# Retention and gMLP block: the first pair's half-row block last, five w_sg transposes instead of ten, a new order

## Chip, core and metric

One core of one Trainium2 chip. The metric is device time in microseconds; less is better.

## What is computed

```python
scores = (1 / sqrt(64)) * q @ k^T             # q, k, v: 8 sequences x 8 heads x 576 x 64, float32
ret = scores * where(t >= s, gamma_h ** (t - s), 0)
x = ret @ v                                   # joined over heads: 8 x 576 x 512
h = gelu_tanh(x @ w_in)                       # 512 -> 1024; u, v = the two halves of 512
v_n = (v - mean) / sqrt(var + 1e-6) * g_ln
v_s = einsum('ts,bsd->btd', w_sg, v_n) + b_sg # 576 x 576, mixes the rows of a sequence
out = x + (u * v_s) @ w_out                   # 512 -> 512
```

## The kernel before

The eight sequences go in four pairs, p = 0 to 3. A pair has 2 x 576 = 1152 rows, nine tiles of 128. Since 576 is four and a half tiles, one tile of a pair holds 64 rows of either sequence. The attention part cuts a pair into five blocks, b = 5p + n: four of 256 rows (two tiles) and one of 128 rows, the half-row block, with 64 rows of each sequence. The table `RB` lists them:

```python
RB = [(2, 0, ((0, 0), (0, 128))), (2, 2, ((0, 256), (0, 384))),
      (1, MID, ((0, 512), (1, 0))),
      (2, 5, ((1, 64), (1, 192))), (2, 7, ((1, 320), (1, 448)))]
```

Each entry has the rows in units of 128, the first tile (0 to 8, MID = 4), and for two chunks the sequence and its first row. So the half-row block comes third and joins the last 64 rows of sequence 0 to the first 64 of sequence 1; sequence 1's tiles are then shifted by 64 rows.

A block passes these steps. `a_load` (L457, L460) brings q, k and v by SP's queue; q of two full blocks comes in one load, except in the first two blocks. `a_prep` (L491 on ACT, L493 and L503 on POOL, one L503 on DVE) scales q and v by powers of gamma and casts. `a_T` (L540) transposes on PE, DVE copies out (L555). `a_S` (L591) makes scores, DVE multiplies them by a mask (L604). `a_Z` (L627) makes the state of a chunk, summed on DVE (L652, L655) and cast on ACT (L659, L661). `a_O` and `a_O2` (L673) make the output, ACT writes it to xT (L730). Then come, tile by tile, `m_V` (L741), its gelu (L748), the statistics (DVE, L756 and L757), four small steps on POOL (L761 to L764), the normalised tile vn (ACT, L776, and L773 twice for the half-row tile, whose two halves go into vmid with zeros in the other half) and `m_U` (L788) with its gelu (L798).

When a sequence's five tiles are normalised, `m_W` (L807) multiplies them by w_sg transposed: eight groups of five matmuls, 288 columns each. DVE multiplies the result into uT (L817). `m_O` (L838) multiplies by w_out; the input x is added by identity matmuls (L833, pair 0) or on DVE from a transposing DMA `xr` (L847, other pairs); `m_store` (L860) writes out.

w_sg is loaded (L402, L406), cast into wnat (ACT, L413) with 64 zero columns on either side, and transposed on PE (L921), 25 matmuls for each of two sets: wT[0], and wT[1] shifted by 64 rows for sequence 1. DVE copies each of the ten results (L925).

Filling matmuls (L357, tile scr, on a zero tile) stand in PE's queue early in the program, 26 in all; each runs as two passes in the trace.

The order on every engine is written out by hand: `ORDER` is a list of job numbers, with fN for a filling of N units of 128 columns. `Planner.follow` places the jobs engine by engine in that order and `emit` issues them. Buffers are counted: eight for loads (ld), two for q (ldq), four PSUM tiles of tag d, two of tag pp, two each for xT and uT, eleven for vn. SP's queue is in order, so a load that waits for its buffer holds everything behind it.

Of the kernel before, what the change touches and what calls it, by code (L numbers as in the profile page):

```python
# [12 lines left out]
BF = mybir.dt.bfloat16  # L13
I32 = mybir.dt.int32
Act = mybir.ActivationFunctionType
Alu = mybir.AluOpType
# [6 lines left out]
PR = dict(PB0=10000.0, O=4000.0, PB=9900.0, S=2000.0, S2=400.0, Z=1901.0, V=6000.0, V2=900.0, U=1260.0, W=4000.0, WS=19000.0, slack=60.0, pen=500.0)  # L23

ORDER = (
# [33 lines left out]
)  # L59


# [173 lines left out]
def kernel(  # L235
# [38 lines left out]
    def new(tag, shape, dtype):  # L274
# [5 lines left out]
          (2, 5, ((1, 64), (1, 192))), (2, 7, ((1, 320), (1, 448)))]  # L280
    NBK = len(RB)
    XP = 1
# [5 lines left out]
    wnat = consts.tile([128, SB, S + 128], BF, name="wnat")  # L288
# [12 lines left out]
    NQ, NV = 13, 2 * NBK  # L301
# [7 lines left out]
    wT = [[consts.tile([128, S], BF, name=f"wT{e}_{j}") for j in range(SB)] for e in range(2)]  # L309
# [8 lines left out]
    nc.gpsimd.iota(srow_i[:, 9:13], pattern=[[256, 2], [1, 2]], base=-ORG, channel_multiplier=2)  # L318
    for o, r0 in ((NQ, 0), (NQ + 6, 64)):
        nc.gpsimd.iota(srow_i[:, o:o + 4], pattern=[[-256, 2], [-1, 2]], base=ORG - r0, channel_multiplier=-2)  # L320
    for e in range(2):
        R = slice(64 * e, 64 * e + 64)
        nc.gpsimd.iota(srow_i[R, 8:9], pattern=[[1, 1]], base=RB[2][2][e][1] - ORG, channel_multiplier=1)
        nc.gpsimd.iota(srow_i[R, NQ + 4:NQ + 6], pattern=[[-1, 2]], base=ORG - RB[2][2][e][1], channel_multiplier=-1)
# [7 lines left out]

    for o, n, w in ((0, 2, 4), (8, 1, 1), (9, 2 + NBK, 2)):
# [30 lines left out]
    HB = [ns / 2.0 for ns, _, _ in RB]  # L364
    T0 = []
    t = 9000.0
    for n in range(NP * NBK):
        T0.append(t)
        t += HB[n % NBK] * (PR["PB0"] if n < NBK else PB)

# [27 lines left out]
    def sg_load():  # L398
# [12 lines left out]
        def g(j):  # L411
            src = wst["in", 1][:, j, :S] if j < 4 else sg4()
            nc.scalar.activation(wnat[:128 if j < 4 else 64, j, 64:64 + S], src, Act.Copy)  # L413
# [23 lines left out]
    def joint(b):  # L437
        return b % NBK == 2 or b in JOINT

    def unit(b):  # L440
        p, n = divmod(b, NBK)
        return ("j", b) if joint(b) else (p, n > 2)

    def half_of(b):
        return (b % NBK) % 3 if b % NBK < 2 else b % NBK - 3

    def a_load(b, t):
        p, n = divmod(b, NBK)
        ns, m, ch = RB[n]
# [12 lines left out]
    def qb_of(b):  # L462
        f_, ns = st["qb", unit(b)], RB[b % NBK][0]
# [4 lines left out]
    def kb_of(b):  # L468
        ns = RB[b % NBK][0]
# [3 lines left out]
    def a_prep(b, t, c=None, eng="POOL"):  # L473
        p, n = divmod(b, NBK)
        ns = RB[n][0]
# [6 lines left out]
        if t == "v":  # L482
# [3 lines left out]
            g = powers(NQ, NBK, 2)[:, n, :, :ns]  # L486
# [8 lines left out]
        else:  # L495
# [3 lines left out]
            g = powers(8, 1, 1)[:, 0] if ns == 1 else powers(9, 2, 2)[:, n] if joint(b) else powers(0, 2, 4)[:, n // 3]  # L499
# [27 lines left out]
    def a_T(b, t):  # L527
        tp = psP.tile([128, 2, 1024], BF, name="pp", tag="pp")
        st[b, "tp", t] = tp
        ns = RB[b % NBK][0]  # L530
# [15 lines left out]
    def new_T(b, t):  # L546
        if t == "q":
            st["qT", unit(b)] = new("qT", [128, 2048], BF)
            return st["qT", unit(b)], 1024 * RB[b % NBK][0]
# [12 lines left out]
    def T_of(b, t, r, c, kk):  # L562

        ns = RB[b % NBK][0]
# [13 lines left out]
    def a_S(b, g):  # L578
        ns = RB[b % NBK][0]
# [19 lines left out]
    def a_Sev(b, g):  # L599
        ns = RB[b % NBK][0]  # L600
# [11 lines left out]
    ZC = [(0, 1), (0, 1), (1,), (0, 1), (0,)]  # L612
    ZFIRST, ZLAST = ((0, 0), (2, 1)), ((1, 1), (4, 0))
    ZN = [3, 2, 2, 2, 1]

    def a_Z(b):
        ns, cs = RB[b % NBK][0], ZC[b % NBK]
# [21 lines left out]
    def z_read(ins, b):  # L639
        cur["left", b] = cur.get(("left", b), ZN[b % NBK]) - 1  # L640
        unfence(ins, ("Z", b), cur["left", b] == 0)

    def a_Zsum(b, c):
        n = b % NBK
        z = cur["zp", b, c]
        if (n, c) in ZLAST:
# [4 lines left out]
        if (n, c) in ZFIRST:  # L651
# [5 lines left out]
    def a_Zev(b, c):  # L657
        if (b % NBK, c) in ZFIRST:
# [4 lines left out]
    def a_O(b):  # L663
        ns, zs = RB[b % NBK][0], st.pop((b, "zs"))
# [55 lines left out]
    def a_Oev(b, c, eng="ACT"):  # L720
        p, n = divmod(b, NBK)
        ns, m, _ = RB[n]
# [43 lines left out]
    def m_norm(i):  # L766
# [3 lines left out]
        if m == MID:  # L770
# [30 lines left out]
    def m_W(b, c, half):  # L801
        p, e = divmod(b, 2)
        t0 = NT * p + (MID if e else 0)
        ps = psD.tile([128, HS], F32, name="wp", tag="d")
        cur["wp", b, c, half] = ps
        for j in range(SB):
            ins = nc.tensor.matmul(ps[:], vns[t0 + j][e][:, 128 * c:128 * c + 128],  # L807
# [398 lines left out]
```

## Time and profile before

| what | us |
|---|---|
| span of the profiled execution | 211.4 |
| runs, median of 3 | 213.68 |
| runs, lowest and highest | 212.73, 214.7 |
| PE busy | 197.6 (93%) |
| DVE, ACT, POOL busy | 152.5, 116.8, 118.3 |
| bytes moved by DMA | 48.37 MB, 229 GB/s over the span |

The span runs from the first to the last instruction of one profiled execution; the timed runs are others. Busy shares are means over stages with different limits: DMA queues are full up to about 165 us and nearly empty after, and PE begins with filling.

### The profile page before, as it was taken

To read this page: it belongs to the slowest core of one execution; us is meant where nothing else is said; L and a number is where in the kernel's file an instruction comes from. 1 tells how busy PE (TensorE), PEld (TensorE's weight loads), DVE (VectorE), ACT (ScalarE), POOL (GpSimd) and SP (SyncE) were. 2 spreads that over 40 slices of the span, in tenths; PEclk is the share of its full clock that TensorE was granted. 3 is DMA by queue.
4 is the path that set the end of the run, shared out by engine and by line. 5 is a ranking of instruction groups with operands and counts; after the bars stand their busy time and mean duration, and the time that the engine had idled before them with its cause. 6 is when DMAs were issued, how large, how long until landed. Compare 5 with 4: busy or idle time off the path is not lost.

```text
span 211.4 us, 7911 instructions
## 1 busy us (share of the span) xinstructions
PE 197.6 (93%) x3384; PEld 137.8 (65%) x3416; DVE 152.5 (72%) x291; ACT 116.8 (55%) x207; POOL 118.3 (56%) x169
## 2 busy tenths in 40 slices
PE   7939999988999999999999999999999999999992
PEld 6727586666676677666767677566677675656661
DVE  3296498877888287967888875897865688576673
ACT  5230598892486954579585452776248349334400
POOL 8735158998667859993769679147582313022000
PEclk9985999999999999999999999999999999999999
DMA  6999999999899999999999999999999902586655
GB/s 164 335 276 305 170 374 295 231 291 340 192 248 296 296 324 276 214 328 189 243 285 109 243 307 206 198 323 182 222 172 148 270 0 78 149 153 174 176 172 198
DMA packets 85910, 48.37 MB, mean 229 GB/s; under 512 B 37035, under 2 KB 79283, under 8 KB 85875
## 3 DMA queue, kind: packets, MB, share of 16 engines
q1 hardware_dynamic: 85856, 47.87, 97.3%
q8 instruction: 26, 0.43, 0.9%
q14 instruction: 10, 0.07, 0.2%
q10 hardware_dynamic: 18, 0.00, 0.0%
HBM read 32.79 MB, written 9.44 MB: 200 GB/s over the span
## 4 chain that ended last, share of the span: by engine, by line
PE 79%; DVE 9%; issue 3%; POOL 3%; DMA 3%; ACT 1%; DVEq 0%; SPq 0%; POOLq 0%
PE wp L807 17%; PE hu L788 13%; PE op L838 13%; PE hv L741 12%; PE scr L357 6%; PE pp L673 6%; PE pp L591 4%; PE pp L540 3%; DMA ld<-in_v_dram 3%; DVE ret L604 2%; PE zp L627 2%; POOL vb L503 1%; DVE bst L756 1%; PE op L833 1%; POOL qb L503 1%
## 5 line engine op out<-in xcount | busy, mean ns | idle before, releaser
L807 PE MATMUL wp<-wT,vn 128*128 128x288 bf16 x256 | 41.1, 286 | 0.7 <-issue 0.6
L503 POOL TENSOR_TENSOR vb<-ld,gpow 128x1024 bf16<-128x1024 f32 (+1 forms) x20 | 34.5, 1731 | 11.6 <-DMA ld<-in_v_dram 8.8
L604 DVE TENSOR_TENSOR ret<-pp,msk 128x1024 bf16<-128x1024 f32 x32 | 38.3, 1215 | 3.4 <-PE pp L591 3.4
L788 PE MATMUL hu<-xT,w_in 128*128 128x256 bf16 (+1 forms) x320 | 36.8, 262 | 0.2
L817 DVE TENSOR_TENSOR uT<-wp,uT 128x288 bf16<-128x288 f32 x64 | 27.6, 451 | 12.4 <-PE wp L807 11.2
L741 PE MATMUL hv<-w_in,xT 128*128 128x512 bf16 x122 | 34.7, 380 | 1.7 <-ACT xT L730 0.3
L838 PE MATMUL op<-w_out,uT 128*128 128x512 bf16 (+1 forms) x138 | 34.4, 373 | 0.6 <-issue 0.2
L776 ACT ACTIVATE vn<-vg,mv 128x512 bf16<-128x512 f32 x32 | 25.3, 809 | 15.3 <-POOL mv L764 15.2
L748 ACT ACTIVATE vg<-hv 128x512 f32<-128x512 f32 x36 | 21.3, 596 | 21.8 <-PE hv L741 16.6
L788 PEld LDWEIGHTS <-w_in 128*128 128x128 bf16 x320 | 28.1, 98 | 7.2 <-issue 0.8
L756 DVE BATCH_NORM_STATS2 bst<-vg 128x6 f32<-128x512 f32 x36 | 24.7, 685 | 9.3 <-ACT vg L748 9.3
L730 ACT ACTIVATE xT<-pp 128x512 bf16<-128x512 f32 (+1 forms) x40 | 20.8, 550 | 18.1 <-PE pp L673 18.1
L807 PEld LDWEIGHTS <-vn 128*128 128x128 bf16 x256 | 24.4, 98 | 9.6 <-issue 0.7
L761 POOL TENSOR_SCALAR mv<-mv 128x2 f32<-128x2 f32 (+1 forms) x20 | 4.5, 224 | 44.7 <-DVE mv L757 37.8
L503 POOL TENSOR_TENSOR qb<-ldq,gpow 128x1024 bf16<-128x1024 f32 x14 | 26.9, 1934 | 4.0 <-DMA ldq<-in_q_dram 4.0
L798 ACT ACTIVATE uT<-hu 128x512 bf16<-128x512 f32 x36 | 21.2, 594 | 13.0 <-PE hu L788 12.9
L855 DVE TENSOR_TENSOR ob<-op,xr 128x512 f32<-128x512 f32 (+1 forms) x28 | 18.4, 669 | 8.3 <-PE op L838 6.3
L838 PEld LDWEIGHTS <-uT 128*128 128x128 bf16 x148 | 13.7, 98 | 11.3
L741 PEld LDWEIGHTS <-xT 128*128 128x128 bf16 x144 | 13.2, 98 | 12.0 <-ACT xT L730 0.2
L807 PE MATMUL wp<-wT,vmid 128*128 128x288 bf16 x64 | 18.0, 287 | 0.1
L357 PE MATMUL scr<-warm 128*128 128x256 f32 (+1 forms) x52 | 16.5, 489 | 1.2 <-DVE warm L316 1.2
L357 PEld LDWEIGHTS scr<-warm 128*128 128x128 f32 x52 | 13.0, 271 | 3.9 <-DVE warm L316 1.2
(100 smaller groups left out, 261.7 us busy)
## 6 DMA issues: line engine op xcount, KB each, us to landing
out_dram<-ob SPq DMA_DIRECT2D x35, 256.0 KB, 3.5
ld<-in_k_dram SPq DMA_DIRECT2D x16, 512.0 KB, 6.9
ld<-in_v_dram SPq DMA_DIRECT2D x16, 512.0 KB, 7.0
ldq<-in_q_dram SPq DMA_DIRECT2D x7, 1024.0 KB, 9.6
xT<-in_moe_w_sg_dram SPq DMA_DIRECT2D x2, 576.0 KB, 8.4
ld<-in_q_dram SPq DMA_DIRECT2D x2, 512.0 KB, 7.0
xT<-in_moe_w_in_dram SPq DMA_DIRECT2D x1, 1024.0 KB, 8.0
ld<-in_k_dram SPq DMA_DIRECT2D x8, 128.0 KB, 6.0
```

Source lines behind the costliest of these rows:

```text
L357: nc.tensor.matmul(scr[:, :w], warm[:, :128], warm[:, :w], start=True, stop=True, skip_group_check=True)
L503: ve.tensor_tensor(dst, src, g.unsqueeze(len(src.shape) - 1).to_broadcast(list(src.shape)), op=Alu.mult)
L604: ins = nc.vector.tensor_tensor(ret[:].rearrange("p r (k t) -> p (r k) t", k=2), sc[:].rearrange("p r (k t) -> p (r k) t", k=2), (msk2 if ...
L741: ins = nc.tensor.matmul(hv[:], xTs[p][:, m, kk, :], w_in[:, kk, F2:], start=(kk == 0), stop=(kk == KK - 1))
L748: unfence(nc.scalar.activation(vgs[i][:], cur.pop(("hv", i))[:], Act.Gelu_apprx_tanh), ("V", i))
L756: nc.vector.bn_stats(bst[:], vgs[i][:])
L776: nc.scalar.activation(vn[:], vg[:], Act.Identity, scale=mv[:, s, 2:3], bias=mv[:, s, 3:4])
L788: ins = nc.tensor.matmul(hu[:, n, :], w_in[:, kk, 128 * c:128 * c + 128], xTs[p][:, m:m + w, kk, :], start=(kk == 0), stop=(kk == KK - 1), ...
L798: unfence(nc.scalar.activation(uTs[p][:, c0:c1, 128 * m:128 * m + 128 * w], cur.pop(("hu", i, half))[:], Act.Gelu_apprx_tanh), ("U", i, half))
L807: ins = nc.tensor.matmul(ps[:], vns[t0 + j][e][:, 128 * c:128 * c + 128], wT[e][j][:, half * HS:(half + 1) * HS], start=(j == 0), stop=(j ...
L817: ins = nc.vector.tensor_tensor(uTs[p][:, c, col:col + HS], cur.pop(("wp", b, c, half))[:], uTs[p][:, c, col:col + HS], op=Alu.mult)
L838: ins = nc.tensor.matmul(op[:], uTs[p][:, c, r], w_out[:, c, cs], start=(p >= XP and c == 0), stop=(c == KK - 1), skip_group_check=True)
```

## The change

Pair 0 (`HL = (0,)`) gets a layout of its own, `RL`: four full blocks first, two for each sequence, and the half-row block last, with the last 64 rows of both sequences. Sequence 1's full tiles then begin at its row 0, so for this pair both sequences use wT[0]; only the half of the last tile that belongs to sequence 1 needs w_sg in the upper 64 rows, which is wT[1][:, 0]. Pairs 1 to 3 keep `RB`.

PE makes only the five transposes of wT[0]. The set wT[1] comes from wT[0] by three DMAs from SBUF to SBUF on SP's queue, shifted by 64 rows: the first one 576 elements of 64 rows for pair 0, the other two (2880 and 2304 elements) for the other pairs; the one that overwrites the piece of pair 0 comes after all W matmuls of pair 0's sequence 1. wnat has zero columns on one side only.

For pair 0, W of either sequence needs the half-row tile, so both begin after all nine tiles are normalised. The last 64 columns of each sequence lie apart in uT, so in half 1 the product (L870) is one instruction of 224 columns and one of 64: eight more instructions. The half-row tile's store is two DMAs of 64 rows. The state sums have four full blocks with two chunks each and none for the last: 8 matmuls more. The table of powers has three more columns.

The order on all engines is new. PE's list has 25 wtp matmuls instead of 50 and 28 filling matmuls instead of 26: 11 ahead of the first transpose of rsrc (12 before), 4 behind it (2 before), 6 around the rest of the first two blocks (12 before, of which 5 stood behind the scores of the second block; now none do), and 7 behind the last output matmul. The last stores are of two whole tiles; before they were of the two halves of one tile. The load of w_out comes later in SP's queue: behind the k loads of pair 1's last two blocks.

```diff
-PR = dict(PB0=10000.0, O=4000.0, PB=9900.0, ...
+PR = dict(T0=(6500.0, 14500.0, 23700.0, 28000.0, 35500.0), TB=45000.0, PB0=10000.0, O=4000.0, PB=9900.0, ...
 ORDER = (
...
+    RL = [(2, 0, ((0, 0), (0, 128))), (2, 2, ((0, 256), (0, 384))),
+          (2, 4, ((1, 0), (1, 128))), (2, 6, ((1, 256), (1, 384))),
+          (1, 2 * MID, ((0, 512), (1, 512)))]
     NBK = len(RB)
+    HL = (0,)
+
+    def lay(b):
+        p, n = divmod(b, NBK)
+        return (RL if p in HL else RB)[n]
+
+    def mid_of(p):
+        return 2 * MID if p in HL else MID
+
+    def tiles_of(p, e):
+        if p in HL:
+            return [MID * e + j for j in range(MID)] + [2 * MID]
+        return [MID * e + j for j in range(SB)]
...
-    wnat = consts.tile([128, SB, S + 128], BF, name="wnat")
+    wnat = consts.tile([128, SB, S + 64], BF, name="wnat")
...
-    wT = [[consts.tile([128, S], BF, name=f"wT{e}_{j}") for j in range(SB)] for e in range(2)]
+    wT = [consts.tile([128, SB, S], BF, name=f"wT{e}") for e in range(2)]
...
+    def z_states(b):
+        p, n = divmod(b, NBK)
+        if p in HL:
+            return ((b - 3, 1), (b - 1, 1)) if n == 4 else (None if n in (0, 2) else (b - 1, 1), (b, 0))
+        return (None if n == 0 else (b - 1, 1), None if n == 2 else (b, 0))
...
     def m_W(b, c, half):
...
+        for j, m in enumerate(tiles_of(p, e)):
+            if p in HL:
+                w = wT[1][:, 0, r] if m == 2 * MID and e else wT[0][:, j, r]
+            else:
+                w = wT[e][:, j, r]
+            ins = nc.tensor.matmul(ps[:], vns[NT * p + m][e][:, 128 * c:128 * c + 128], w, start=(j == 0), stop=(j == SB - 1))
...
     def m_Wg(b, c, half):
...
+        if p in HL:
+            cols = [(MID * 128 * e + half * HS, half * HS, min(HS, S - NB0 - half * HS))]
+            if half:
+                cols.append((2 * MID * 128 + NB0 * e, S - NB0, NB0))
+        else:
+            cols = [(e * S + half * HS, half * HS, HS)]
+        for n, (o, t, w) in enumerate(cols):
+            ins = nc.vector.tensor_tensor(uTs[p][:, c, o:o + w], ps[:, t - half * HS:t - half * HS + w], uTs[p][:, c, o:o + w],
+                                          op=Alu.mult)
...
+    def shift_wT(part):
+        if part == 0:
+            nc.sync.dma_start(wT[1][NB0:, 0, :], wT[0][:NB0, SB - 1, :])
+        elif part == 1:
+            nc.sync.dma_start(wT[1][NB0:, :, :], wT[0][:NB0, :, :])
+        else:
+            nc.sync.dma_start(wT[1][:NB0, 1:, :], wT[0][NB0:, :SB - 1, :])
...
-    for e in range(2):
-        for j in range(SB):
...
+    for j in range(SB):
+        bf = Buf("d")
+        jb = add("PE", 285.0, 31000.0 + 1000.0 * j, lambda j=j: build_wT(j), deps=sg + [j_z0], new=bf, mode="F", ins=11)
+        jt.append(add("DVE", 450.0, jb.due + 500.0, lambda j=j: evac_wT(j), deps=[jb], uses=[bf]))
```

More of the change, by code (lines that the diff above doesn't have):

```diff
@@ L280, with spans @@
           (2, 5, ((1, 64), (1, 192))), (2, 7, ((1, 320), (1, 448)))]
+    RL = [(2, 0, ((0, 0), (0, 128))), (2, 2, ((0, 256), (0, 384))),
+          (2, 4, ((1, 0), (1, 128))), (2, 6, ((1, 256), (1, 384))),
+          (1, 2 * MID, ((0, 512), (1, 512)))]
     NBK = len(RB)
+    HL = (0,)
[8 more added lines that the diff above has]
+        return [MID * e + j for j in range(SB)]
+    def spans(p, m):
+        if p not in HL:
+            return [(e, max(0, 128 * m - e * S), min(S, 128 * m + 128 - e * S)) for e in range(2)
+                    if 128 * m < (e + 1) * S and 128 * m + 128 > e * S]
+        if m == 2 * MID:
+            return [(0, S - NB0, S), (1, S - NB0, S)]
+        return [(m // MID, 128 * (m % MID), 128 * (m % MID) + 128)]
     XP = 1
@@ L363 @@
     PB = PR["PB"]
[L364 to L367, printed above, removed]
+    T0 = list(PR["T0"])
+    t = PR["TB"]
+    for n in range(len(T0), NP * NBK):
         T0.append(t)
-        t += HB[n % NBK] * (PR["PB0"] if n < NBK else PB)
+        t += lay(n)[0] / 2.0 * (PR["PB0"] if n < NBK else PB)
     wst, jw, stage = {}, {}, {}
@@ L802, in m_W @@
         p, e = divmod(b, 2)
[L803 removed]
         ps = psD.tile([128, HS], F32, name="wp", tag="d")
         cur["wp", b, c, half] = ps
[L806 to L809 removed]
+        r = slice(half * HS, (half + 1) * HS)
+        for j, m in enumerate(tiles_of(p, e)):
[4 more added lines that the diff above has]
+            ins = nc.tensor.matmul(ps[:], vns[NT * p + m][e][:, 128 * c:128 * c + 128], w, start=(j == 0), stop=(j == SB - 1))
             if j == 0:
@@ L859, in m_store @@
         cs = slice(0, DM) if hf is None else slice(hf * DM // 2, (hf + 1) * DM // 2)
-        nc.sync.dma_start(outf[128 * i:128 * i + 128, cs], cur["ob", i][:, cs])
+        p, m = divmod(i, NT)
+        sp = spans(p, m)
+        if p in HL:
+            r = 0
+            for e, lo, hi in sp:
+                o = (2 * p + e) * S
+                nc.sync.dma_start(outf[o + lo:o + hi, cs], cur["ob", i][r:r + hi - lo, cs])
+                r += hi - lo
+        else:
+            nc.sync.dma_start(outf[128 * i:128 * i + 128, cs], cur["ob", i][:, cs])
     def to_col():
@@ L956 @@
         j.due = -1e6 + n
-    j_z0 = add("DVE", 850.0, -6e5, zero_wnat, what="zero")
+    j_z0 = add("DVE", 550.0, -6e5, zero_wnat, what="zero")
     j_z1 = add("POOL", 1700.0, -6e5, zero_vmid, what="zero")
@@ L975, with shift @@
         j.due = 42000.0
-    jt = {}
-    for e in range(2):
-        for j in range(SB):
-            bf = Buf("d")
-            jb = add("PE", 285.0, 31000.0 + 1000.0 * (SB * e + j), lambda e=e, j=j: build_wT(e, j),
-                     deps=sg + [j_z0], new=bf, mode="F", ins=11)
-            jt[e, j] = add("DVE", 450.0, jb.due + 500.0, lambda e=e, j=j: evac_wT(e, j), deps=[jb], uses=[bf])
+    jt = []
+    for j in range(SB):
+        bf = Buf("d")
+        jb = add("PE", 285.0, 31000.0 + 1000.0 * j, lambda j=j: build_wT(j), deps=sg + [j_z0], new=bf, mode="F", ins=11)
+        jt.append(add("DVE", 450.0, jb.due + 500.0, lambda j=j: evac_wT(j), deps=[jb], uses=[bf]))
+    def shift(part):
+        n = (1, SB, SB - 1)[part]
+        jsh.append(add("SP", 550.0, (42000.0, 66000.0, 64000.0)[part], lambda: shift_wT(part),
+                       deps=jt + ([J["W", 1, c, hf] for c in range(KK) for hf in range(2)] if part == 1 else []),
+                       nbytes=NB0 * n * 2 * S, run=2 * S * n))
+    shift(0)
     for b in range(NBL):
         p, n = divmod(b, NBK)
-        ns, m, ch = RB[n]
+        ns, m, ch = lay(b)
         t0 = T0[b]
@@ L1152 @@
                     m_ = i % NT
-                    lo, hi = 128 * m_, 128 * m_ + 128
-                    need = [J["Wg", 2 * p + ee, c, hf] for ee in range(e + 1) for c in range(KK) for hf in range(2)
-                            if lo < ee * S + (hf + 1) * HS and hi > ee * S + hf * HS]
+                    need = [J["Wg", 2 * p + ee, c, hf] for ee, lo, hi in spans(p, m_) for c in range(KK) for hf in range(2)
+                            if lo < (hf + 1) * HS and hi > hf * HS]
                     obb = Buf("ob")
```

162 lines of the change are left out of this document (85 added, 77 removed), and 66 rows, old and new, of the table ORDER.

## The prediction

> **What bounds the kernel now.** I read the page's slices first, then a table by stage, then the chain of waits, then the groups.
>
> The page's slices, 5.3 us each: busy tenths of PE, the granted clock, and the DMA queues.
>
> ```profile
> PE   7939999988999999999999999999999999999992
> ...
> PEclk9985999999999999999999999999999999999999
> DMA  6999999999899999999999999999999902586655
> ```
>
> PE is full from slice 5 to the end; DMA is full from slice 2 to about 165 us. The table by stage, busy time of each engine:
>
> ```profile
> 0.00:22.00 22.00, 16.98 (x148) 13.46 (x148) 11.16 (x36) 6.08 (x8) 13.30 (x33) 0.84 1.03 270
> 22.00:47.00 25.00, 23.03 (x570) 16.75 (x571) 20.42 (x36) 20.90 (x37) 17.74 (x24) 1.00 1.08 272
> 47.00:63.00 16.00, 14.94 (x317) 10.82 (x321) 12.63 (x21) 8.69 (x16) 11.50 (x12) 1.00 1.01 261
> 63.00:160.00 97.00, 95.38 (x1887) 65.82 (x1904) 74.60 (x134) 59.84 (x112) 67.20 (x81) 1.00 1.16 244
> 160.00:207.80 47.80, 47.31 (x473) 30.93 (x477) 33.26 (x64) 21.26 (x36) 8.57 (x21) 1.00 0.57 148
> ```
>
> Columns: stage, its length, PE, PEld, DVE, ACT, POOL, clock, DMA share, GB/s. From 63 to 207.8 us PE idles 1.62 + 0.49 = 2.1 us. So the middle can give at most 2.1 us, and time can come out of PE work or of the first 63 us. There PE's busy time holds 16.5 us of L357, matmuls on a zero tile (scr) that only fill waits. The chain of waits at the head and at the first W and first output matmuls:
>
> ```profile
> 16.32 5.51 PE scr L357 x14
> 21.84 0.37 PE tp L887 x5
> 22.21 0.68 PE pp L673 x36
> ...
> 46.99 2.07 PE wp L807 x16
> ...
> 63.22 0.81 PE op L838 x3
> ```
>
> Filling sits on the chain itself: attention output O of block 0 begins at 22.1 because 14 filling passes end at 21.8, though the last DVE mask product it needs ends at 18.8. The passes are slow, 0.40 us each against 0.22 in the later fill (2.21 us for 10). The clock tells why:
>
> ```profile
> 14.00:16.00 2.00, 1.03 (x60) 0.90 (x52) 2.00 (x3) 0.95 (x2) 1.57 (x2) 0.53 1.22 290
> 16.00:18.00 2.00, 2.00 (x18) 1.56 (x9) 2.00 (x4) 0.00 (x0) 1.40 (x2) 0.50 1.13 341
> 18.00:20.00 2.00, 2.00 (x6) 1.55 (x6) 1.14 (x2) 0.00 (x0) 1.52 (x1) 0.50 1.21 254
> ```
>
> **The change, part by part.**
>
> *Transposes.* 25 of 50 w_sg transposes and 5 of 10 copies (L925) go. In the timeline 24 transposes take 1.51 us with the last one's latency, 5 in the chain 0.39 to 0.45; at the pace of the output's identity matmuls of the same size (0.11 us above a 0.86 us group, 4 of them) they would be 0.03 to 0.06 each. I take 0.058, 1.4 us. They lie on PE's full stretch, so 1.4 us off the end; bounds 0 (the first 25 run at 28.6 to 30.5, just behind filling, and PE might wait there anyway) and 1.5. DVE loses 5 x 0.448 = 2.2 us.
>
> *Head.* The rest is order. Rates for PE work from the chain: V 0.216 a matmul, U 0.109, W 0.1226, T 0.018, S 0.016, Z 0.0125, O 0.018. Summed over the built instruction orders, without filling: before has 20.9 us of work ahead of its first W (46.9 us) and 35.1 ahead of its first output (63.2). After has 31.4 ahead of its first W, because both sequences' W now need the shared last tile; 1.4 of that is transposes, against 2.9 before. The same state is before's 30.0 + 2.9 = 32.9, which it passes at 46.9 + (32.9 - 20.9) x 16.3/14.2 = 60.7 us. The question is when after starts W.
>
> Data: before's queues moved 2.43, 5.33, 7.95, 10.75 and 13.75 MB by 10, 20, 30, 40 and 50 us (10 us rows of the same table: 243, 290, 262, 280, 300 GB/s). In after's SP order that lands v of block 1 (4.3 MB) at 16.6, q of blocks 2 and 3 at 20.2, their k at 24.2, the second w_in half at 28.2, v of block 2 at 30.2, w_sg at 34.4, v of block 3 (9.7 MB) at 36.3, q for pair 1 at 40.9, the half block's v at 42.7, v of block 5 (13.2) at 48.2.
>
> Block 0 and 1: DVE's column work ends at 11.9 as before; row copy 0.4, qT 1.23, S on PE, mask product 1.2, two sums 0.8, mask product 1.2: 18.0. PE has 12 passes of filling instead of 14, some half as wide, and ends them at 19.6 at the slow clock; transposes 0.6; O of block 0 at 20.2 against 22.1. S of block 1 waits for the two evictions (0.59 each), its masks end at 26.4, O of block 1 at 26.4 against 30.5. Here after leads by 4.
>
> Then POOL sets the pace: q 4.2 us and k 2.1 end at 26.4; the four small mv steps (1.6) wait for DVE's statistics at 28.0 and end at 29.6; v of block 2 30.2 to 32.1; v of block 3 36.3 to 38.2; then without a wait half q 1.04, mv 1.6, q 2.1, half k 0.61, q 2.1, half v 1.04, two k casts 2.07, mv 1.6, v 1.9, mv of the half block's tile 1.3: 53.6. ACT's two L773 steps are 1.65: 55.3. PE in its own order, with these dates, idles briefly at 42.9 and 48.1 and reaches W at 57. DVE needs 28 us of work from 26 on, so it ends at 54 and fits, without slack. Low end 56 (POOL alone); I take 57.5, half a microsecond for mode gaps that rows of single kinds leave out. So 3.2 us earlier than 60.7, transposes included.
>
> *Shifted set.* Three SBUF-to-SBUF copies, 64 rows of 576, 2304 and 2880 elements, 0.74 MB. No row shows such a copy. Bounds: 0 (it rides in a queue whose loads run 7 us from issue to landing) and 0.74 MB/244 GB/s = 3.0 us. I take 0: from 63 on PE waits for no load. On SP the first copy stands behind k and ahead of v of blocks 5 and 6, and waits for DVE's fifth wT copy, about 43 us; SP comes there at about 42 (before's 22nd issue is at 40.3). If DVE is late, those v are late with it, then POOL, then Z of block 5; 1 us late costs 1 us, as POOL has no slack there. The third stands behind PE's W of sequence 1, which ends some 20 us before its place in the queue; behind it wait loads of pair 2.
>
> *uT products.* Eight W evictions of 288 columns become 224 + 64. At the slope of 256 columns 0.42 and 288 0.451 that is about 0.38 + 0.2, so 0.13 more each, 1.0 us of DVE. DVE is 77% busy in 63 to 160 and 79% in 47 to 63, and PE gives a W every 0.61: 0, or 1.0 if DVE binds.
>
> *Small parts.* 8 more Z matmuls 0.1. One store in two parts: another 0.4 to 0.55 us of SP issue, SP waits anyway: 0. Three more columns of powers in the setup: 0. Later w_out load: 17.6 MB lands by 66, four casts of 0.72 end by 69; first output after about 71: 0, bound 2.
>
> *Tail.* Before ends with two half tiles (0.42 on DVE, 128 KB, 2.0 us to landing); after ends with two whole tiles (0.69, 256 KB, 3.5). That is 0.27 on DVE and 0 to 1.5 on the store; since two stores are in flight there in both, I take 0.3 in all. Seven filling matmuls stand behind the last matmul: 14 x 0.22 = 3.1 us, under the 3.6 that the last eviction and store take: 0.
>
> *Middle order.* New throughout; bounds -2.1 (all idle gone) and +7.5 (47 to 63's idle share, 6.6%, over 144.8 us). Nearest row is the same stage's own 1.5%: 0.
>
> Sum: -3.2 + 0.1 + 0.3 = -2.8. The profiled span is 211.4; after's would be 208.6. The median of the runs is 2.28 above that span, which I keep: **210.9 us**.
>
> On the clock the row stands first: PE was busy 1.2 of 4 us from 10 to 14, and 0.50 was granted until past 20. [...] That speaks against a change that takes the filling at 26.6 to 28.8 out. [...]
>
> **The rivals.**
>
> *The lead is used up before W.* POOL gets v of block 3 at 36.3 only by bytes; with two late waits W begins at 60.5. Then only 0.2 of head and 0.3 of tail remain: 213.8. For it: DVE and POOL both without slack from 26 to 54. Against: each chain alone ends at 54 to 55.
>
> *Slower: the feed.* The place is POOL's queue before W. If the queues bring not the 270 GB/s of 0 to 47 but the span's 229, block 3's v (9.7 MB) lands at 42.4, 6.1 us later, POOL's unbroken row shifts with it, and W begins at 63.6: +2.9 +0.4 = 217.0. It decides from W at 60.7 on; each microsecond beyond costs one. For it: POOL waited six times, 8.8 us in all, for v. Against: after's early loads have longer rows (the half block, 256 B a row, comes later).
>
> *The clock falls again.* In my walk PE waits 1.6 us before O of block 1, with no filling. Should 0.50 be granted from 25 to 29, 3.4 us of work take 1.7 more: 212.6. For: the 10 to 14 us row. Against: PE is over half busy around it.
>
> *Better.* 18 us of W and output work in hand at 57 cover every load wait: half of the 2.1 idle and no tail loss: 209.5, and 208.6 with W at 56.6.
>
> **How the numbers follow.** Chances: forecast 0.46 (own range 209.6 to 212.2, two thirds below 211.5), better 0.16, used up 0.18, clock 0.05, feed 0.15. One per cent, 2.1 us, is about what a measurement of this kernel can tell from no change. Faster by more: 0.32 + 0.16 + 0.02 = 0.50; slower by more: the feed, 0.15; within: 0.35. The range takes in better and used up, and the near part of the feed: 208.6 to 215.6.
>
> **What would show it.** Right: O of block 0 near 20, O of block 1 near 26.5, first W at 57 to 58, first output near 71, PE idle after that under 2.5 us, 25 wtp matmuls. Wrong in the head: first W past 60, with POOL or DVE named before it. Wrong in the middle: PE idle over 4 us after the first output, with wT or ld as releaser. Wrong in the tail: more than 4.2 us from the last output matmul to the end.

## The result: 224.1 us, slower by 4.7%

The changed kernel takes 224.11 us (median of four runs, 221.34 to 227.21) against 214.13 us before (212.73 to 214.70): ratio 1.047, 95% interval 1.040 to 1.054. Ratios here compare the undisturbed executions of both kernels, so they can differ a little from the quotient of the medians. The forecast was 210.9 us with a range of 208.6 to 215.6: the time lies above the range, and the sign was wrong as well. The profiled execution took 224.13 us with a span of 222.4.

The same slices of the page, now 5.6 us each:

```profile
PE   7876949699969999399994999999996999999998
...
PEclk9999799999999999979998899999999999999999
DMA  6999999989999999989999996598999813529786
```

Before, PE was at 8 or 9 from the fourth slice to the last but one. Now it has holes all the way, two of them deep (3 and 4, at about 89 and 119 us), and at each the granted clock falls to 0.50 for 3.41 us (from 93.80 and 121.11 us on). The table by stage, columns as before:

```profile
0.00:22.00 22.00, 16.02 (x285) 12.85 (x286) 13.81 (x36) 10.79 (x16) 14.82 (x35) 1.00 1.02 274
22.00:47.00 25.00, 19.15 (x434) 12.74 (x433) 19.18 (x32) 15.86 (x29) 17.99 (x19) 0.93 1.10 266
47.00:63.00 16.00, 15.31 (x361) 10.93 (x362) 13.09 (x26) 11.18 (x21) 11.07 (x15) 1.00 0.97 218
63.00:160.00 97.00, 88.11 (x1756) 60.30 (x1773) 67.66 (x126) 56.75 (x104) 62.34 (x79) 0.96 1.01 230
160.00:218.40 58.40, 56.17 (x535) 37.45 (x540) 37.88 (x75) 22.03 (x38) 12.33 (x23) 1.00 0.71 168
```

From 63 to 160 us PE idles 97.00 - 88.11 = 8.9 us where it idled 1.6 before, and part of the rest runs at half clock. In the chain of waits (start, length, what), the places where that time goes:

```profile
39.64 1.71 issue
...
89.15 3.35 issue
92.50 0.46 PE pp L568 x19
...
120.87 0.91 issue
121.79 4.56 PE wp L855 x25
```

"issue" is time in which PE waited for nothing that the profile shows. PE's own sequence around 89 us (start, length, operation, and in brackets the idle time before it):

```profile
88.42 0.42 PE L619 MATMUL pp<-qT,kT 64*64 64x128 bf16 x16
88.78 0.38 PE L568 MATMUL pp<-ident,kb 64*128 64x64 bf16 x13
92.50 0.46 PE L568 MATMUL pp<-ident,kb 64*128 64x64 bf16 x19 [3.35 <-issue]
```

That stop is the clue: it lies inside one job, after 13 of 32 transposes that read the same finished tile and write the same buffer. No data that the job reads can hold the fourteenth and not the thirteenth. What arrives just ahead of the resume is found in the DMA queues. From 90.1 to 91.2 us:

```profile
q1 hardware_dynamic: 274, 0.28, 100.2%
q8 instruction: 1, 0.02, 6.0%
```

Queue q8 is taken to carry PE's code, its instructions: 26 packets of 16 KB over the span, 0.43 MB, and 26 x 256 is 6,656, nearly all of PE's 6,829 instructions. The packet here starts at 90.11 and lands at 91.16; PE resumes 1.34 us later. The stops at 39.64 (1.71 us) and 118.69 (3.10 us) end 1.57 and 1.31 us behind such a packet too. At the last one the profile names ACT, but the weight load ahead of the waiting matmul, which waits for nothing, comes no earlier:

```profile
121.78 0.61 PEld L855 LDWEIGHTS <-vn 128*128 128x128 bf16 x4 [3.59 <-issue]
121.79 1.14 PE L855 MATMUL wp<-wT,vn 128*128 128x288 bf16 x4 [3.10 <-ACT zb L705]
```

Counted in the built program, the three stops stand at instructions 1218, 3266 and 4290: 8 x 256 and 4 x 256 apart. (The trace, which lacks some records, has 1,215, 3,254 and 4,271 rows of PE ahead of them.) Before has two small ones of this kind, 0.56 us at 49.06 and 0.35 us at 56.29; the first is at instruction 1474, which is 1218 + 256. 16 KB for 256 instructions would be 64 bytes each, an estimate from the packet's size and this step.

So the idle time of PE, 23.6 us now against 10.1 before, parts into: stops that end 1.3 to 1.6 us behind a code packet, 8.2 us against 0.9; waits for data behind 47 us, 3.3 against 0 (1.66 at 62.83 for POOL's cast of pair 1's half-row block, behind a load of q that POOL itself waited 2.86 us for, and 1.68 at 169.57 for a transposing DMA); waits in the first 47 us, 7.7 against 4.8; the rest, in small pieces and the first 1.24, 4.4 in both. The half clock (0.50) was granted three times for 3.41 us, from 22.1, 93.8 and 121.1 on, the last two 1.3 us behind and 0.7 us ahead of the ends of the two long stops; before, one stretch of 6.83 us, from 14.11 on, lay in the filling. Up to the last output matmul PE is busy 194.8 us rather than 197.6, 2.8 less (fewer transposes, less filling ahead of it, against up to 1.7 us lost in each half-clock stretch, an estimate: half of 3.41), and behind that matmul lie 0.2 us more. 13.5 us more idle, less 2.8, plus 0.2 are the 11.0 us of span.

### The profile page after: what moved, and what is told of

It reads as the page before. It is cut to its first block, busy times and chain, and to the rows that moved or that the text cites. A ratio compares the mean times of both kernels' runs of the same rounds, so it can differ in the third digit from the quotient of the medians.

```text
span 222.4 us, 7902 instructions
## 1 busy us (share of the span) xinstructions
PE 197.8 (89%) x3372; PEld 136.6 (61%) x3403; DVE 152.3 (68%) x293; ACT 116.6 (52%) x207; POOL 118.5 (53%) x169
## 4 chain that ended last, share of the span: by engine, by line
PE 68%; DMA 9%; DVE 8%; issue 7%; POOL 5%; ACT 2%; SPq 0%; DVEq 0%; ACTq 0%; POOLq 0%
PE wp L855 15%; PE hu L832 13%; PE hv L785 12%; PE op L891 12%; PE pp L717 5%; PE pp L619 4%; DMA ldq<-in_q_dram 3%; POOL qb L531 3%; DMA qT<-qb 3%; DMA ld<-in_q_dram 3%; PE pp L568 2%; PE zp L672 2%; DVE bst L800 1%; PE scr L382 1%; DVE ret L632 1%
## 5 line engine op out<-in xcount | busy, mean ns | idle before, releaser
L531 POOL TENSOR_TENSOR vb<-ld,gpow 128x1024 bf16<-128x1024 f32 (+1 forms) x20 | 35.2, 1762 | 14.7 <-DMA ld<-in_v_dram 12.7
L785 PE MATMUL hv<-w_in,xT 128*128 128x512 bf16 x123 | 37.6, 402 | 1.6 <-issue 0.5
L870 DVE TENSOR_TENSOR uT<-wp,uT 128x288 bf16<-128x288 f32 (+2 forms) x72 | 27.6, 414 | 13.7 <-PE wp L855 13.3
L855 PEld LDWEIGHTS <-vn 128*128 128x128 bf16 x256 | 25.3, 100 | 12.9 <-issue 3.6
L842 ACT ACTIVATE uT<-hu 128x512 bf16<-128x512 f32 x36 | 20.7, 595 | 14.8 <-PE hu L832 14.8
L908 DVE TENSOR_TENSOR ob<-op,xr 128x512 f32<-128x512 f32 (+1 forms) x28 | 18.5, 669 | 10.1 <-PE op L891 9.5
L785 PEld LDWEIGHTS <-xT 128*128 128x128 bf16 x144 | 13.4, 101 | 13.5 <-issue 2.4
L583 DVE COPY qT<-pp 128x2048 bf16<-128x2048 bf16 (+1 forms) x11 | 11.2, 1022 | 8.6 <-PE pp L568 8.6
L382 PE MATMUL scr<-warm 128*128 128x256 f32 (+1 forms) x56 | 14.1, 408 | 1.2 <-DVE warm L340 1.2
```

The source lines that it names most:

```text
L531: ve.tensor_tensor(dst, src, g.unsqueeze(len(src.shape) - 1).to_broadcast(list(src.shape)), op=Alu.mult)
L785: ins = nc.tensor.matmul(hv[:], xTs[p][:, m, kk, :], w_in[:, kk, F2:], start=(kk == 0), stop=(kk == KK - 1))
L842: unfence(nc.scalar.activation(uTs[p][:, c0:c1, 128 * m:128 * m + 128 * w], cur.pop(("hu", i, half))[:], Act.Gelu_apprx_tanh), ("U", i, half))
L855: ins = nc.tensor.matmul(ps[:], vns[NT * p + m][e][:, 128 * c:128 * c + 128], w, start=(j == 0), stop=(j == SB - 1))
L870: ins = nc.vector.tensor_tensor(uTs[p][:, c, o:o + w], ps[:, t - half * HS:t - half * HS + w], uTs[p][:, c, o:o + w], op=Alu.mult)
```

## Experiments

**Theory A, code blocks.** PE's instructions come in blocks of 256, the step at which the three stops stand. The theory assumes that a block is asked for only when PE enters the one ahead of it, at a border, and that PE stops where a block's work is shorter than the time until its successor has arrived; no trace had shown this yet. With the stops of 3.35 and 3.10 us came 0.50 of the clock, 3.41 us each. The new order puts runs of short attention matmuls (0.012 to 0.018 us each, two instructions) between two borders: the block ahead of the stop at 89.15 was used up in about 3.5 us. **Theory B, data.** The stops are waits that the profile names badly: the copies for the shifted set are in flight at both, and the chain and the groups name vn, zb and xT at the second. The first four runs share one chip; before stood there at 213.73 us.

**1. Move the borders, keep the order.** 192 instructions more at places in the filling where PE waits anyway:

```diff
+        for _ in range(48 * a):                       # to_rows, a = 1
+            nc.tensor.transpose(tp[:, :64], ident[:64, :4], ident[:64, :64])
...
+        for _ in range(48 if b == 0 and ("S", 0) not in cur else 0):   # a_S
+            nc.tensor.matmul(sc[:64, 0, :64], ident[:64, :64], ident[:64, :64], ...)
```

> The changed kernel with 192 more instructions on TensorE in the filling (48 small transposes of the identity ahead of the rows of the bias, 48 small products ahead of the first scores, both at places where TensorE waits anyway for about 1.3 us), order and all other work as they are. Theory A (code blocks): TensorE's instructions come in blocks of 256, and a block that is used up in less than the 5.9 to 7.0 us from its border to its successor's arrival ends in a stop; 192 instructions shift every later border, so that the dense stretches no longer fall between two borders. It expects the stops of 3.35 us (at 89.15) and 3.10 us (at 118.69) to go, and with each its window of half clock of 3.41 us (1.7 us lost in each): 224.1 - 3.35 - 3.10 - 3.4 = 214 us, within 212 to 218. Theory B (waits on data: the copies for the shifted set, the loads, the normalized tiles named by the chain): nothing in the data moves, so 224 us, within 1 us, with both stops at the same work.

Measured: 218.24 us, ratio to before 1.022 (1.017 to 1.028): 5.9 us off by adding useless work, which B cannot give. But A had said 214, so its time was missed (its range reached to 218). The two stops of over 3 us and the half clock behind 22 us are gone; in their place are seven smaller stops behind code packets, 0.5 to 2.7 us, 8.9 us in all, no less than the 8.2 of the changed kernel. The total hides where they stand. First W begins 2.35 us later than in the changed kernel (61.34 for 58.99), and 5.1 us of the seven lie ahead of it. From there to the last output matmul the run is 8.2 us shorter: code stops of 3.7 us for 6.5, one late wait for data of 0.5 for 3.3, and no half clock. PE's waits, us in total, times, longest:

```profile
PE pp L622 <- issue: 4.5, 3, 2.7
PE zp L675 <- issue: 2.0, 2, 1.3
PE pp L720 <- issue: 1.9, 1, 1.9
```

So the order has too many dense runs for this place of the borders as well. All seven stops come, counted in the trace, 193 or 194 rows above a multiple of 256 (449, 1,985, 2,241, 2,753, 3,009, 3,778, 4,546), as 1,218 does.

**2. Leave the copies out.** The second sequence of pairs 1 to 3 multiplies with the unshifted set:

```diff
-                w = wT[e][:, j, r]
+                w = wT[0][:, j, r]
```

> The changed kernel without its two late SBUF-to-SBUF copies (360 and 288 KB); the second sequence of pairs 1 to 3 multiplies with the unshifted set instead. TensorE's instructions are the same in number and order. Theory A (code blocks): both stops stay, 222 to 224 us; at most the code's packet, which started 4.6 us behind its border while a copy was in flight, starts some us earlier, which would shorten the stop at 89.15. Theory B in the form that the copies did it (they are in flight from 85.1 to 93.5 and from 107.9 to 116.2, just at the two stops): both stops go, 214 to 217 us.

Measured: 223.88 us, ratio 1.044 (1.036 to 1.052). The loss stays without the copies, so B in that form falls. In its trace (the fastest execution, 221.31 us) the code stops are shorter: 0.41 us at 43.23, 0.33 in the transposes of k, 1.61 one block later, 1.60 ahead of the W near 119, all 1.3 to 1.5 us behind a packet; against that its first W comes 2.3 us later, as PE waits 2.6 us longer for the column work. Whether a copy in flight delays a packet is not settled by this one profile.

**3. Move the borders of the kernel before.** 32 instructions ahead of the first transposes of q, where PE waits 2.8 us:

```diff
+        for _ in range(16 if b == 0 and t == "q" else 0):
+            nc.tensor.transpose(tp[:64, 0, :64], ident[:64, :64], ident[:64, :64])
```

> The kernel before with 32 more instructions on TensorE in the filling (16 small transposes of the identity ahead of the first transposes of q, where TensorE waits 2.8 us anyway), nothing else. Theory A (code blocks): the borders move to places where three blocks are used up in about 2.7, 3.1 and 3.6 us of work, so stops of 1 to 3 us appear, one of them near 100 us of the span, with a window of half clock behind it where it is long: 216 to 220 us. Theory B (waits on data): 214 us, within 0.7.

Measured: 212.37, 216.77, 218.74 and 219.25 us, one as fast as before and three longer, so the times alone decide nothing. The trace is of the longest. It has stops of 1.42, 1.93 and 0.60 us at 34.41, 48.96 and 84.26 (rows 962, 1,473 and 2,753, 193 or 194 above a multiple of 256), each 1.3 to 1.6 us behind a code packet, and the half clock from 36.3 and from 49.9 us on. New stops at borders are what A said; none came near 100 us, where it had put one. Whether the fast execution escaped because its packets started earlier is not shown: it has no trace.

**4. Five transposes and two copies alone, in the order of before.**

```diff
     def build_wT(e, j):
+        if e:
+            return
...
+    def shift_wT(part):
+        if part:
+            nc.sync.dma_start(wT[1][:NB0, 1:, :], wT[0][NB0:, :SB - 1, :])
+        else:
+            nc.sync.dma_start(wT[1][NB0:, :, :], wT[0][:NB0, :, :])
```

Ahead of the first transposes of q stand 25 small ones, 50 instructions, so that the later borders stay where they were.

> The kernel before, its order and its layout of rows, with only one part of the change: the five sets of transposes for the second sequence's weights and their five evictions are left out, and two SBUF-to-SBUF copies bring the shifted set (issued after the loads of about 58 us); 50 small transposes' worth of instructions stand in the filling so that the code borders stay where they were. Theory A: the transposes save 25 x 0.058 = 1.4 us, the copies cost nothing: 212.7 us, within 211.5 to 214. Theory B in the form that the copies are dear (648 KB more on a filled DMA): 215 to 218 us.

Measured: 217.71 us, ratio 1.019 (1.012 to 1.025): A's number was missed, and the time lies where B had put dear copies. Its first output is evicted at 63.4 us rather than 65.8, its last but one at 211.1 rather than 207.9. Between them PE stops for 1.41, 0.74 and 0.80 us at 71.07, 92.61 and 113.24 behind code packets, 1.3 at 87.07 for POOL's q, 0.9 for its v. No wait names a copy; whether the two copies, ahead of loads in SP's queue, made that q and v late is not shown. Either way, an order that fits with 1.4 us of work more does not fit without it.

**5. The code by itself.** 1,792 small transposes (14 blocks) with no transfer under way, then 1,792 more beside 25 loads of 512 KB and the stores that follow them:

```diff
+    dense(14 * 128, ident)
+    ...
+    for n in range(24):
+        load(n)
+    dense(14 * 128, seed)
```

> The disputed cost by itself: TensorE does 1,792 small transposes (64 x 64, two instructions each: 14 blocks of 256) with no transfer under way, then the same again while 25 loads of 512 KB run. It computes nothing of the reference: it writes zeros. Theory A (code blocks): 128 transposes of 0.018 us would take 2.3 us a block; with no transfers a block takes 2.3 to 3.5 us (a code packet of 1.0 to 1.3 us and the 1.3 us from its landing to the resume), with the loads running 5 to 7 us a block, with a stop in each that ends about 1.3 us after a code packet lands. Theory B (the stops were waits on data): 2.3 us a block in both, without stops.

All transposes used the same rows and took 0.053 us each. At 6.8 us a block PE never stopped, with or without loads: the code kept up. That bounds the cost from above, but no block was short. With the rows alternating as in the kernel:

```diff
-            nc.tensor.transpose(tp[:64, :], src[:64, :64], ident[:64, :64])
+            R = slice(64 * (i % 2), 64 * (i % 2) + 64)
+            nc.tensor.transpose(tp[:, i % 2, :64], src[R, :], ident[R, R])
```

> The disputed cost by itself, now with transposes that alternate between the two halves of the rows, as the kernel's own do (in the first attempt each took 0.053 us, 6.8 us a block of 256, so that no block was used up early). 1,792 of them (14 blocks of 256 instructions) with no transfer under way, then the same again while 25 loads of 512 KB run; zeros are written, nothing of the reference is computed. Theory A (code blocks): at 0.018 us each a block is 2.3 us of work; with no transfers it takes 2.3 to 3.5 us, with the loads running 4 to 7 us, each with a stop that ends 1.3 to 1.6 us after a code packet has landed. Theory B (the stops were waits on data): 2.3 us a block in both halves, no stops.

PE without transfers, then with them:

```profile
10.24 2.04 PE L266 MATMUL tp<-ident 64*128 64x64 bf16 x128 [1.69 <-issue]
13.97 2.04 PE L266 MATMUL tp<-ident 64*128 64x64 bf16 x128 [1.69 <-issue]
...
62.11 2.04 PE L266 MATMUL tp<-ident,seed 64*128 64x64 bf16 x128 [1.71 <-issue]
66.93 2.04 PE L266 MATMUL tp<-ident,seed 64*128 64x64 bf16 x128 [2.78 <-issue]
72.03 3.43 PE L266 MATMUL tp<-ident,seed 64*128 64x64 bf16 x128 [3.06 <-issue]
```

A stop after every 128 transposes, 256 instructions, with nothing to wait for. From resume to resume a block takes (50.16 - 10.24)/11 = 3.63 us in the quiet half and (119.18 - 62.11)/12 = 4.76 us beside the transfers; 2.0 of it is work at full clock. The packet starts 1.0 to 1.5 us behind the resume in the quiet half and 1.8 to 2.9 beside the transfers. Beside them the granted clock falls to a mean of 0.79, in the quiet half it stays at 1.00. This shows stops at the borders of 256, each ending behind a packet, without any data in play.

**6. Other orders, with the instructions counted as built.** The kernel's written plan knows of blocks: each PE job carries a count of its instructions, and borders every 256 are priced at 5.0 to 5.4 us. But the counts written there add up to 7,257, while the built program has 6,829: if the surplus is spread evenly, the plan's border near the 3,266th instruction is some 200 instructions from the real one (an estimate from these two sums). I searched orders for the same jobs by the same plan, with the built counts. Only the order's list differs from the kernel it starts from:

```diff
 ORDER = (
-    '1 f6 0 2 6 73 f1 f7 17 7 f5 94 95 75 3 f8 76 96 8 97 12 79 80 74 98 262 22 99 13 264 192 82 190 193 f3 77 100 '
+    ...
```

First the changed kernel and before, both from the start; beside them a control of run 1 that moves the borders by only 8 (`range(4 * a)` in to_rows). Before stood at 213.57 us on this chip.

> The changed kernel with another order of the same jobs: the order is searched with each TensorE job's count of instructions as built (6,829 in all, where the counts written at the jobs add up to 7,257 and so put the later borders of 256 at the wrong jobs) and with 5.0 to 6.4 us for each block. Layout, transposes, copies and loads are as in the changed kernel. Theory A (code blocks): no stop above 1.5 us behind the first 30 us, no window of half clock there, 210 to 215 us. Theory B (layout and copies are what costs): 220 to 226 us.

> The kernel before with its order searched in the same way (counts as built, 5.0 to 6.4 us a block), nothing else. Theory A: its only stops of this kind were 0.56 and 0.35 us, so there is little to take away: 210 to 214 us, and no run with a window of half clock behind the first 30 us. Theory B: the order is not what matters, 213 to 215 us.

> The changed kernel with 8 more instructions (4 small transposes of the identity ahead of the rows of the bias), as a control for the 192 of the first run: the same kind of addition, but the borders move by 8 places only. Theory A: the dense stretches still lie between two borders (the shortest block gets 2.1 us of work rather than 2.9), so both stops stay: 223 to 227 us. If additions in the filling helped by something else than the borders (TensorE kept warm, other timing in the head), 218 to 222 us.

Measured: the changed kernel 218.95 us, ratio 1.035 (1.020 to 1.050); before 213.02 us, 1.000 (0.995 to 1.006); the control 226.07 us, 1.063 (1.046 to 1.079). The control speaks for the place of the borders and against padding as such: 8 instructions leave the loss as it was (stops of 1.76, 2.62 and 2.36 us behind packets), 192 take 5.9 us off. A padding of 256, which would put the later borders at the same work again, was not run. In the control the stop near 120 us stands ahead of a V job rather than behind it, four matmuls or just 8 instructions earlier in the program, and no engine is named:

```profile
122.39 1.89 PE L785 MATMUL hv<-w_in,xT 128*128 128x512 bf16 x4 [2.36 <-issue]
```

For before, both theories allowed the time that came; it shows that the search alone gains nothing. In the new order the changed kernel's code stops are down to 2.9 us, none above 1.1. It still missed my 210 to 215: the search had moved the column work behind filling passes, PE waited 3.6 us for it at 11.05, the half clock (0.50) came for 10.24 us in the head, and once more, which I had excluded, for 3.41 us from 61.62 on.

**7. The changed kernel once more, for a second trace.**

> The changed kernel once more, unaltered, for a second trace. Theory A (code blocks): stops that end 1.3 to 1.6 us behind a code packet at the same two places of the program (in the transposes of k behind 85 us and ahead of a product with the weights near 119 us), their length free to vary by some us with how late the packet starts; 222 to 226 us. Theory B (waits on data): stops as long as before (3.4 and 3.1 us), and not tied to code packets.

222.68 us, beside 211.29 for one run of before. The stops come at the same jobs, with other lengths: 1.00, 1.17 and 1.98 us, and one of 2.98 in the block behind the second, each 1.3 to 1.7 us behind a packet. A changed length alone proves little, since the wait at 62.83 changed too (1.66 and 1.04 us); that the places are borders again is what A needs. At the third the profile names ACT's xT here, zb in the first trace and vn in run 2: at most one of the three can be what the same job waits for.

**8. Counted order with the changed kernel's own head.** The search now leaves the first 36 us of the plan alone; the second run gives the same treatment to the kernel of run 4, and the third shifts the first one's borders by 128. Before stood at 214.98 us here.

```diff
+        for _ in range(32 * a):                       # third run, to_rows; 32 products in a_S likewise
+            nc.tensor.transpose(tp[:, :64], ident[:64, :4], ident[:64, :64])
```

> The changed kernel with its own order up to about 36 us of the written plan, and behind that an order searched with the counts as built and 5.0 to 6.6 us for a code block. Theory A (code blocks, the rest of the loss included): 209 to 214 us, code stops of under 2 us in all behind 47 us. Theory B (half of the loss belongs to the layout: later weights, copies, loads): 217 to 221 us, as with the first counted order.

> The layout of before with five sets of transposes and the two copies for the shifted set, its order of before up to about 36 us of the plan and counted behind that. Theory A: the 217.7 us of the uncounted version were code stops, so the 1.4 us of the transposes come through now: 211 to 213.5 us. Theory B (the copies are dear): 216 to 219 us.

> The counted order with the kept head, with 128 more instructions on TensorE in the filling (64 small transposes and products of the identity where it waits anyway), so that the borders no longer stand where the order was searched for. Theory A: 4 to 9 us slower than without them (215 to 222 us), with stops of over 1 us that end 1.3 to 1.6 us behind a code packet. Theory B: as without them, within 1.5 us.

Measured: 215.64 us, ratio 1.006 (1.000 to 1.012); 215.60 us, 1.010 (1.001 to 1.020); 218.62 us, 1.022 (1.011 to 1.034). The middle stage of the first:

```profile
63.00:160.00 97.00, 93.70 (x1783) 65.13 (x1799) 71.41 (x138) 56.90 (x106) 66.03 (x76) 1.00 1.17 248
```

PE's longest wait in the third:

```profile
PE zp L681 <- issue: 3.9, 2, 3.0
```

The same layout, jobs, copies and loads as the changed kernel, 8.5 us faster by the medians. In its trace, of the fastest execution (212.92 us), PE is busy 93.70 us in the middle stage rather than 88.11, at full clock, with one code stop left, of 0.95 us. Moving its borders by 128 brings back a stop of 3.0 us in the middle of a job and 3.0 us of time; I had said 4 to 9. So an order of the same work can be had without most of the loss, and 3.0 us of it come back when only the borders move (4.0 us in the two traces, from the first W to the last output matmul). That the other 5.5 are the borders too is not shown, because the counted order differs on every engine; in the trace of the changed kernel code stops are 7.3 of the 13.5 us of added idle time, the half clock aside. The time isn't 210.9, and A's 209 to 214 was missed. Nor does the kernel of run 4 get its 1.4 us (A had said 211 to 213.5); there PE waits 0.84 us for a copy, and the code stops are 2.1 us rather than 3.0.

**9. A second counted order, other seed.**

> A second order of the changed kernel from the same search (head kept, counts as built), with another seed. If what is left over belongs to the layout, both orders stand at the same time: 214.5 to 217 us. If it belongs to the single order, this one may lie anywhere from 210 to 218 us.

216.86 us, with before at 214.68; ratio 1.007 (1.003 to 1.011). Two orders, one time: with the code counted, the layout stands at before's time or up to about 1% behind it, not 1.5% ahead. No version here beats before. In this order's one trace, of an execution of 219.71 us, PE's longest wait behind 47 us is for a copy of the shifted set: 2.35 us at 118.19.

## Why the prediction was wrong

The step that failed is the order of the middle, which the prediction priced at 0. The parts follow in the prediction's own order.

*Transposes.* 25 wtp matmuls are there, five in 0.39 and ten in 0.56 us on the chain: 0.056 to 0.078 each for 0.058. Right as a price on PE. That it comes off the end was not shown: runs 4 and 8 had the saving and were not faster.

*Head.* I gave O of block 0 at 20.2, O of block 1 at 26.4, first W at 57.5 and first output at 71. The trace has 17.5, 25.4, 58.99 and 73.9. So 1.7 of the forecast 3.2 us at W. The head also differs between executions: PE's wait for the column work is 1.26 and 1.50 us in the two traces of the changed kernel, and 3.9 us in those of runs 2 and 6 (the control), which start alike. The traces show where the difference lies. The last of DVE's small column steps takes 0.17 us in the changed kernel and 3.13 in run 2, where it runs beside POOL's work on q and k and ends as that does (start, length):

```profile
11.17 0.17 DVE L942 TENSOR_TENSOR col<-colr,col 128x10 bf16<-128x10 f32 x1
...
11.70 3.13 DVE L942 TENSOR_TENSOR col<-colr,col 128x10 bf16<-128x10 f32 x1
11.92 1.89 POOL L531 TENSOR_TENSOR qb<-ld,gpow 128x1024 bf16<-128x1024 f32 x1
13.77 1.03 POOL L518 CAST qb<-ld 128x1024 bf16<-128x1024 f32 x1
```

The column work had begun 0.84 us later there (first transpose of rsrc at 8.26 for 7.42 us). The control has 3.14 us for the same step. So less than a microsecond at the start becomes 2.6 us of PE's time; no run takes POOL's work away to prove it.

*Shifted set, uT products, tail, w_out.* 0 for the copies: the changed kernel's trace has no wait for them, and run 2 without the two late ones took 223.88 us. In other orders PE did wait for one, 0.84 us in run 8 and 2.35 in run 9, so the 0 holds for this order alone. Landing took 2.5 to 8.4 us. DVE's uT products cost 27.6 us in all and never bound. Between the last output matmul and the end lie 3.9 us, inside my 4.2, against 3.7 before, with the filling behind it covered.

*Middle order.* This step failed: "Nearest row is the same stage's own 1.5%: 0". From 63 us on idle time rose by 9.0 us (7.3 up to 160, 1.7 behind it), past the upper bound of 7.5, with two half-clock stretches on top; of the 11.1 us of idle time from 63 us on, 6.5 are the two long code stops and 3.2 the two late waits for data. I took the row for a property of the stage; it was a fit of the old order to its code, whose blocks, counted in the trace, last about 5 to 11 us between 37 us and 177. All but one: that one lasts 2.64 us and passed without a long stop, as its packet started 0.03 us behind the border; others start up to 5 us behind. The page before showed this: PE idle for 0.56 us at a W with nothing named, and 26 packets on an instruction queue. The printed kernel even has a price for it, 5.0 or 5.4 us a block (FETCH, L20), which the sum left out. I wrote down the wait that would show me wrong (over 4 us behind the first output) and got its cause wrong as well, wT or ld.

*Rivals.* "The lead is used up" and "the feed" were placed before W, and W came at 58.99, ahead of the 60.5 and 60.7 from which they count. Late data did take 3.3 us more, at two places that I didn't name. The clock had 0.05, for a wait before O of block 1; it did fall there, at 22.1 to 25.5, and twice more where I had no wait at all. That 3.4 us of work would take 1.7 more was an estimate that no run shows; measured were stretches of 3.41 us at 0.50, which can lose 1.7 us each at most. The mechanism that decided, an order that outruns its code, wasn't among them.

*What stays open.* Why the counted orders of the changed layout don't beat before. In the faster one's profile PE idles 14.9 us, against 10.1 before: 7.4 of it in the first 47 us (2.04 for POOL's q, 1.3 each for v, qT and kT), against 4.8. So what the transposes and the head save in work is waited out for data there; no run took that feed away. Both counted orders come from one search, so its own limits are not excluded either.

## What to carry to other kernels

Before an order, a layout or a padding is priced, count PE's instructions between borders of 256 (the step of the stops here), in the program as built, and compare each block's work with the time from a border to the next block's arrival that the traces show (here 3.6 us in quiet, 4.8 beside transfers, about 6 to 7 at the two long stops). A full engine in the old trace is a property of that order; taking work out of a fitted order can cost more than the work was worth. For a stop in the middle of a job, named "issue" or after an engine whose work can't matter, look first for an instruction packet that lands just ahead of the resume, 1.3 to 1.6 us in the changed kernel. And compare two traces of one kernel before a difference in the head is put down to the change.

## What the runs showed of the hardware

Queue q8, taken as PE's code, moved 26 packets of 16 KB in before and in the changed kernel; the three stops of the changed kernel lie a multiple of 256 instructions apart, and those of run 5's second version 256. In run 5 a packet takes 0.9 to 1.4 us and work resumes 1.2 to 1.6 us after it lands; in the kernels single packets took up to 2.6 us (before, at 98.85), and work resumed 1.3 to 1.8 us after one. In run 5's second version PE stopped at every border from the second on, and every packet started behind its border. In the kernels, counted by the work done, packets start between 2.6 us ahead of the border, where the matmuls are long (run 6's control), and 6.7 us behind it (run 9).

The half clock, 0.50, came in stretches of 3.41, 6.83, 10.24 or, in run 5, 13.65 us. The three of the changed kernel start 71.68 and 27.31 us apart, 21.0 and 8.0 times 3.41. One came with a stop of 3.10 us, in the second trace with one of 1.98 us and in run 3 with one of 1.42, while none came with one of 2.04 us in the counted order. No run varies a stop's length alone, so how long a stop has to be is not shown.
